# Scores of batches 1 to 3 in quarters of 32 queries over 136 keys, in 64x32 tiles of the array, with the global keys laid between the local ones

## Chip, cores and metric

The kernel runs on one core of one Trainium2 chip. The metric is device time in microseconds for one execution, the median over runs. Lower is better.

## What is computed

Local attention with a few global keys, and behind it a gated two-layer network that also mixes positions:

```python
batch, n_heads, seq, head_dim = (4, 8, 768, 64)
n_global, n_local = (8, 96)
scores = scale * np.matmul(q, k.transpose(0, 1, 3, 2))
rel = pos[:, None] - pos[None, :]
is_global = pos[None, :] < int(n_global)
is_local = (rel >= 0) & (rel < int(n_local))
dist = np.where(is_global & ~is_local, float(n_local), np.abs(rel).astype(np.float32))
scores = np.where(is_global | is_local, scores - slopes * dist, -1000000000.0)
a = np.exp(scores - np.max(scores, axis=-1, keepdims=True))
x = np.matmul(a / (np.sum(a, axis=-1, keepdims=True) + 1e-09), v)
h = np.maximum(x @ w_in, 0.0)
u, v = (h[..., :d_ff // 2], h[..., d_ff // 2:])
v_n = (v - mu) / np.sqrt(var + 1e-06)
v_s = np.einsum('ts,bsd->btd', w_spatial, v_n) + b_spatial[None, :, None]
return (u * v_s) @ w_out
```

A query sees the 8 global keys and the 96 keys up to itself.

## The kernel before

The work is cut into 24 blocks n of 128 queries: 4 batches b of 6 blocks i. Everything is resident in on-chip memory apart from the block's q, k and v, which SP's queue loads (`prep`, L767, and `prep_v`, L785).

For each block, `scores` (L799) multiplies q by k in fp32. A head has 64 channels, and two heads lie on the upper and the lower 64 partitions, so the array is used as four 64x64 tiles: 64 channels by 64 queries (`halves`). A half of 64 queries sees 168 columns of k (`KW`): 64 + 96 local keys and 8 global ones, which stand first for the upper half and last for the lower. The first block of a batch (i = 0) has 128 columns. One block is 16 calls: 4 pairs of heads, 2 halves of queries, 2 heads. They fill four PSUM banks `s`. Then `tensor_tensor_reduce` on DVE adds the bias (`bias`, made in `setup_bias` and its inner function `more`, L674, with huge negative entries for keys that a query must not see) and takes the minimum, and ACT does the exponential.

In batches 1 to 3 the probabilities of the next block are transposed (`turns_of`, in 64-partition tiles of 104 or 128 columns, into `s` banks), copied to `pth`, and multiplied with v (`values`, `p<-pth,vring`, four 64x64 tiles). Scores of the block after that mostly stand right behind the values. In batch 0 the transposes are full 128-wide ones. The network's matmuls (`mlp_v`, `mlp_u`, `mlp_s`, `mlp_o`, all written to PSUM tiles `m`) use the whole 128x128 array. They fill the time in which DVE and ACT work on a block's probabilities.

The order of all of it is made at build time: a recorder (`Recorder`, `Engine.keep`, whose line L45 every recorded instruction carries) collects the operations, and `plan` orders them per engine by a table of ranks (`KEYS`) and by costs per operation (`cost`, `shape_of`, `lengths`). `shape_of` (L283) gives PE's tile shape a number and a cost for entering it. `keep_warm` puts dummy transposes (`m<-ident` and the like) into PE's early gaps.

Of the kernel before, what the change touches and what calls it, by code (L numbers as in the profile page):

```python
# [282 lines left out]
def shape_of(op):  # L283

    if op.eng != "tensor":
        return 0, 0
    if op.call != "together":
        return 0, 149 if op.call == "transpose" else 190
    if op.args[-1][0] == "transpose":
        return 3, 145  # L290
    return (1, 135) if list(op.args[-1][2]["lhsT"].ap)[0][1] <= HALF else (2, 150)


def lengths(op):
# [225 lines left out]
def attn_then_spatial_gating_kernel(  # L520
# [47 lines left out]
    k_own = k[:, :, :, :, KP:KP + P]  # L568
# [76 lines left out]

    def setup_bias():
# [610 lines left out]
```

## Time and profile before

| what | us |
|---|---|
| median of 3 runs (lowest, highest) | 427.72 (427.56, 427.98) |
| the profiled execution's own time | 426.2 |
| its span, first to last instruction | 424.4 |
| PE busy (share of the span) | 411.9 (97%) |
| DVE busy | 284.9 (67%) |
| ACT busy | 196.7 (46%) |
| POOL busy | 91.1 (21%) |

The profiled execution is 1.5 us shorter than the median of the runs, and 1.8 us of its time lie outside the span. PE's records of matmuls overlap, since they are pipelined, so its busy share says that it seldom stood empty and not that it ran at its peak. An fp32 matmul call leaves two records on PE, each with a weight load on PEld: a block's 16 score calls are 32 records. The network's matmuls leave one record each.

### The profile page before, as it was taken

To read this page: it belongs to the slowest core of one execution; us is meant where nothing else is said; L and a number is where in the kernel's file an instruction comes from. 1 tells how busy PE (TensorE), PEld (TensorE's weight loads), DVE (VectorE), ACT (ScalarE), POOL (GpSimd) and SP (SyncE) were. 2 spreads that over 40 slices of the span, in tenths; PEclk is the share of its full clock that TensorE was granted. 3 is DMA by queue.
4 is the path that set the end of the run, shared out by engine and by line. 5 is a ranking of instruction groups with operands and counts; after the bars stand their busy time and mean duration, and the time that the engine had idled before them with its cause. 6 is when DMAs were issued, how large, how long until landed. Compare 5 with 4: busy or idle time off the path is not lost.

```text
span 424.4 us, 11946 instructions
## 1 busy us (share of the span) xinstructions
PE 411.9 (97%) x4845; PEld 365.9 (86%) x4845; DVE 284.9 (67%) x1010; ACT 196.7 (46%) x606; POOL 91.1 (21%) x123
## 2 busy tenths in 40 slices
PE   7899899999999999999999999999999999999994
PEld 6667798998898889899889888899989889899993
DVE  7999998679777776748877727658578423524240
ACT  5689675555636552556553525633353222311111
POOL 2355244731000052320010012241010023410000
PEclk9999999999999999999999999999999999999999
DMA  7998555233434530434462314404041010000102
GB/s 236 404 388 300 209 194 178 98 124 102 169 123 146 178 103 21 148 88 144 134 200 78 136 37 148 148 3 145 14 155 61 26 49 2 2 2 2 74 2 82
DMA packets 18885, 51.46 MB, mean 121 GB/s; under 512 B 1924, under 2 KB 4228, under 8 KB 18180
## 3 DMA queue, kind: packets, MB, share of 16 engines
q1 hardware_dynamic: 18820, 50.60, 34.7%
q8 instruction: 40, 0.66, 0.6%
q14 instruction: 25, 0.20, 0.2%
HBM read 44.30 MB, written 6.29 MB: 119 GB/s over the span
## 4 chain that ended last, share of the span: by engine, by line
PE 86%; DVE 10%; ACT 2%; issue 1%; DMA 0%; SPq 0%; DVEq 0%; ACTq 0%
PE m L45 70%; PE s L45 9%; PE p L45 8%; DVE pth L45 4%; DVE pr L45 2%; DVE w_in_l L45 1%; ACT pr L45 1%; DVE w_in_h L45 1%; DVE ev L45 1%; DVE c L45 0%; DMA nraw<-in_n_local_dram 0%; DVE bias L45 0%; DVE xtl L45 0%; DVE rc L45 0%; ACT w_t_h L45 0%
## 5 line engine op out<-in xcount | busy, mean ns | idle before, releaser
L45 ACT ACTIVATE pr<-pr,mn 128x168 f32<-128x168 f32 (+1 forms) x192 | 80.0, 418 | 10.5 <-DVE mn L45 10.3
L45 DVE CUSTOM_DVE_ANT_0 pr<-s,bias 128x168 f32<-128x168 f32 (+1 forms) x192 | 51.3, 319 | 13.3 <-ACT c L45 7.2
L45 ACT ACTIVATE ev<-m 128x512 f32<-128x512 f32 (+1 forms) x40 | 23.5, 589 | 59.2 <-PE m L45 50.5
L45 ACT ACTIVATE gh<-ev 128x384 fp32r<-128x384 f32 x32 | 16.8, 525 | 54.6 <-DVE ev L45 54.5
L45 DVE TENSOR_TENSOR ev<-m,b_bc 128x384 f32<-128x384 f32 x32 | 17.8, 556 | 35.1 <-PE m L45 35.1
L45 PE MATMUL m<-w_t_h,vnh 128*128 128x384 f32 x192 | 40.0, 340 | 0.0
L45 PE MATMUL m<-w_t_l,vnh 128*128 128x384 f32 x192 | 39.8, 337 | 0.0
L45 PE MATMUL p<-pth,vring 64*64 64x64 f32 (+4 forms) x1968 | 39.4, 221 | 0.0
L45 DVE TENSOR_SCALAR pr<-pr,rc 128x168 f32<-128x168 f32 (+1 forms) x134 | 38.7, 345 | 0.6
L45 PE MATMUL m<-w_t_h,vnl 128*128 128x384 f32 x192 | 39.0, 336 | 0.0
L45 PEld LDWEIGHTS p<-pth,vring 64*64 64x64 f32 (+3 forms) x1968 | 36.0, 135 | 2.8 <-issue 0.7
L45 POOL TENSOR_TENSOR vnl<-ev,vnh 128x512 fp32r<-128x512 f32 x24 | 31.2, 1301 | 29.0 <-ACT vnh L45 13.6
L45 DVE BATCH_NORM_STATS2 st<-ev 128x6 f32<-128x512 f32 x24 | 16.5, 690 | 29.7 <-ACT ev L45 29.5
L45 ACT ACTIVATION_READ_ACCUMULATOR pr<-pr,mn 128x1 f32 x192 | 36.0, 188 | 0.0
L45 PEld LDWEIGHTS m<-w_t_h,vnh 128*128 128x128 f32 x192 | 33.7, 188 | 1.5 <-issue 1.2
L45 PEld LDWEIGHTS m<-w_t_l,vnh 128*128 128x128 f32 x192 | 34.1, 188 | 0.3
L45 PEld LDWEIGHTS m<-w_t_h,vnl 128*128 128x128 f32 x192 | 34.0, 188 | 0.2
L45 PE MATMUL s<-k,q 64*64 64x168 f32 (+1 forms) x768 | 32.5, 306 | 0.6 <-DMA k<-in_k_dram 0.5
L45 ACT ACTIVATE u<-m 128x384 f32<-128x384 f32 x28 | 13.7, 491 | 37.3 <-PE m L45 37.2
L45 PE MATMUL m<-w_out_h,gh 128*128 128x512 f32 (+1 forms) x96 | 31.0, 397 | 0.0
L45 ACT ACTIVATE pth<-s 104x512 f32<-104x512 f32 (+2 forms) x37 | 17.6, 531 | 28.5 <-PE s L45 28.0
L45 PE MATMUL m<-w_out_l,gh 128*128 128x512 f32 (+1 forms) x96 | 29.8, 390 | 0.0
(117 smaller groups left out, 788.4 us busy)
## 6 DMA issues: line engine op xcount, KB each, us to landing
vring<-in_v_dram SPq DMA_DIRECT2D x15, 768.0 KB, 4.4
k<-in_k_dram SPq DMA_DIRECT2D x20, 480.0 KB, 5.7
q<-in_q_dram SPq DMA_DIRECT2D x24, 256.0 KB, 4.0
out_dram<-ev SPq DMA_DIRECT2D x23, 256.0 KB, 2.0
vring<-in_v_dram SPq DMA_DIRECT2D x5, 1024.0 KB, 5.1
u<-in_moe_w_in_dram SPq DMA_DIRECT2D x6, 512.0 KB, 6.7
gh<-in_moe_w_spatial_dram SPq DMA_DIRECT2D x6, 384.0 KB, 7.5
k<-in_k_dram SPq DMA_DIRECT2D x4, 256.0 KB, 4.4
```

The costliest lines, as they stand in the source:

```text
L45: getattr(self.real, call)(*args, **kw)
```

## The change

Past the first batch (b > 0) and past the first block of a batch (i > 0), which makes 15 of the 24 blocks, the scores are taken in quarters of 32 queries (`fours`), each with 136 columns (`QW`), in eight 64x32 tiles. A block has 32 calls in place of 16. For that the host lays the 8 global keys between the local ones (`GAT` says where), so that a quarter's keys are one run of columns: the first or the last 136 of its half's 168. The bias and the rows of v are laid in the same way. The 32 columns that a quarter leaves out hold what was there before, and the bias masks them. DVE and ACT still read 168 columns. k gets a second copy of a block's own keys in memory, so that the load for a batch's first block is one contiguous run per partition. `shape_of` knows a fifth tile shape, and the table of ranks is new.

```diff
+KALL = KW + HALF + NGMAX
+GAT = (HALF, KP - NGMAX)
+QW = KW - 32
...
-    return (1, 135) if list(op.args[-1][2]["lhsT"].ap)[0][1] <= HALF else (2, 150)
+    w = op.args[-1][2]["lhsT"]
+    if elements(w) < HALF:
+        return 4, 135
+    return (1, 135) if list(w.ap)[0][1] <= HALF else (2, 150)
...
-    tiles = 4 if shape_of(op)[0] == 1 else 2
+    tiles = {1: 4, 2: 2, 4: 8}[shape_of(op)[0]]
+    if tiles == 8:
+        return [4 * elements(kw["rhs"]) * .417 / tiles + 1 for _, _, kw in op.args]
...
-KEYS = {'start': -756.31, ('P', 0): -243.7, ('bias', 0): -495.76, ...
+KEYS = {'start': -867.27, ('P', 0): -293.52, ('bias', 0): -457.54, ...
...
-    k_own = k[:, :, :, :, KP:KP + P]
+    k_own = k[:, :, :, NP * KALL:].rearrange("n t p (g c) -> n t p g c", c=P)
...
+    halves = [slice(64 * j, 64 * j + 64) for j in range(2)]
+    fours = [slice(32 * j, 32 * j + 32) for j in range(4)]
...
-            ts(out=rel[HALF:P], in0=rel[HALF:P], scalar1=-float(HALF + NGMAX), scalar2=None, op0=ALU.add)
+            for ps, cs, by in ((halves[0], slice(0, GAT[0]), NGMAX), (halves[1], slice(0, GAT[1]), HALF + NGMAX), (halves[1], slice(GAT[1], KW), HALF)):
+                ts(out=rel[ps, cs], in0=rel[ps, cs], scalar1=-float(by), scalar2=None, op0=ALU.add)
             kept(far, rel)
-            nc.vector.tensor_copy(out=far[0:HALF, 0:NGMAX], in_=glob[0:HALF, 0:NGMAX])
-            nc.vector.tensor_copy(out=far[HALF:P, KW - NGMAX:KW], in_=glob[HALF:P, 0:NGMAX])
+            for ps, at in zip(halves, GAT):
+                nc.vector.tensor_copy(out=far[ps, at:at + NGMAX], in_=glob[ps, 0:NGMAX])
...
-        nc.load(out=kt[:, :, cs], in_=k[b, i, :, :, cs])
+        if i:
+            nc.load(out=kt, in_=k[b, i, :, 0:NP * KALL].rearrange("p (g c) -> p g c", c=KALL))
+        else:
+            nc.load(out=kt[:, :, KP:KP + P], in_=k_own[b, i])
...
+        if b and i:
+            where = [(zs, los[y // 2], (KW - QW) * (y % 2), QW) for y, zs in enumerate(fours)]
+        else:
+            where = [(zs, lo, 0, W) for zs, lo in zip(halves, los)]
...
-                    ("matmul", (sp[x // 2 * 2 + j][zs, x % 2],), dict(
-                        lhsT=qt[s_, g + x, zs], rhs=kt[s_, g + x, lo:lo + W], start=True, stop=True,
+                    ("matmul", (sp[x // 2 * 2 + j][zs, x % 2, at:at + w],), dict(
+                        lhsT=qt[s_, g + x, zs], rhs=kt[s_, g + x, lo + at:lo + at + w], start=True, stop=True,
                     ))
-                    for x in range(PAIRS) for zs, lo in zip(halves, los) for j, s_ in enumerate(halves)
+                    for x in range(PAIRS) for zs, lo, at, w in where for j, s_ in enumerate(halves)
```

The first place is PE at one of the 15 blocks (n = 17): the last values (`p<-pth,vring`, out of `values`), the first scores (`s<-k,q`), the last scores and the first matmul of the network (`m<-`). Before, in calls:

```order
L45 MATMUL p_1_118<-pth_3_128,vring_0_92 64x64
L45 MATMUL p_1_118<-pth_2_127,vring_0_92 64x64
L45 MATMUL s_0_100<-k_1_115,q_1_114 64x168
L45 MATMUL s_1_101<-k_1_115,q_1_114 64x168
...
L45 MATMUL s_2_104<-k_1_115,q_1_114 64x168
L45 MATMUL s_3_105<-k_1_115,q_1_114 64x168
...
L45 MATMUL m_1_135<-w_t_h_72,vnh_0_133 128x384
```

With the change:

```order
L49 MATMUL p_1_118<-pth_3_128,vring_0_92 64x64
L49 MATMUL p_1_118<-pth_2_127,vring_0_92 64x64
L49 MATMUL s_0_100<-k_1_115,q_1_114 32x136
L49 MATMUL s_1_101<-k_1_115,q_1_114 32x136
...
L49 MATMUL s_2_104<-k_1_115,q_1_114 32x136
L49 MATMUL s_3_105<-k_1_115,q_1_114 32x136
...
L49 MATMUL m_1_135<-w_t_h_72,vnh_0_133 128x384
```

The two rows of a pair of banks alternate: 8 calls into `s_0` and `s_1` and 8 into `s_2` and `s_3` before, 16 and 16 now. What stands ahead of and behind them is the same. In 11 of the 15 blocks the scores follow values directly, as here, and in 4 a matmul of the network; it is 11 and 4 in both kernels.

The second place is PE at the end of batch 0: the last scores of the first block of batch 1 (n = 6, `s<-k,q`, 128 columns) and the values of block 4 before, of block 5 now. Before:

```order
L45 MATMUL s_2_104<-k_0_94,q_0_93 64x128
L45 MATMUL s_3_105<-k_0_94,q_0_93 64x128
L45 MATMUL m_0_129<-xth_0_116,w_in_h_68 128x384 x4
L45 MATMUL m_0_129<-xtl_0_117,w_in_h_68 128x384 x4
...
L45 MATMUL m_1_135<-xth_0_116,w_in_l_69 128x384 x4
L45 MATMUL p_0_87<-pth_3_128,vring_0_92 64x64 x2
```

With the change:

```order
L49 MATMUL s_2_104<-k_0_94,q_0_93 64x128
L49 MATMUL s_3_105<-k_0_94,q_0_93 64x128
L49 MATMUL p_1_118<-pth_2_127,vring_0_92 64x64 x2
L49 MATMUL p_1_118<-pth_0_119,vring_0_92 64x64 x2
L49 MATMUL p_1_118<-pth_2_127,vring_0_92 64x64 x2
```

Before, 24 matmuls of the network stood between these scores and the next values; now the values follow at once, in the same 64x64 tiles. Elsewhere in batch 0 as many stretches of scores or values stand between matmuls of the network as before.

The third place is DVE at the start, in `setup_bias` (`ev` holds distances, `nf` and `nwide` the two sizes that are loaded). Before:

```order
L45 TENSOR_SCALAR ev_2_97<-ev_0_95 128x128
L45 TENSOR_SCALAR ev_0_95<-ev_0_95 64x168
L45 TENSOR_SCALAR ev_1_96<-ev_2_97 128x128
L45 TENSOR_TENSOR ev_2_97<-ev_2_97,ev_1_96 128x128
L45 CAST nf_64<-nraw_63 128x4
```

With the change:

```order
L49 TENSOR_SCALAR ev_2_97<-ev_0_95 128x128
L49 TENSOR_SCALAR ev_0_95<-ev_0_95 64x64
L49 TENSOR_SCALAR ev_1_96<-ev_2_97 128x128
L49 TENSOR_SCALAR ev_0_95<-ev_0_95 64x96
L49 TENSOR_TENSOR ev_2_97<-ev_2_97,ev_1_96 128x128
L49 TENSOR_SCALAR ev_0_95<-ev_0_95 64x72
L49 CAST nf_64<-nraw_63 128x4
```

One operation on 64x168 has become three, all ahead of the cast that waits for the loaded sizes. From there DVE's rows are the same up to its 108th operation without the readings of minima (33 us in the trace before), and up to the 145th but for one copy that stands later (52 us). Behind that, operations of batch 0 change places.

## Rows read from the trace of the kernel before

**Rows 1.** Page, parts 1 and 2: PE's busy time, and the granted clock by slices.

```profile
PE 411.9 (97%) x4845; PEld 365.9 (86%) x4845; DVE 284.9 (67%) x1010; ACT 196.7 (46%) x606; POOL 91.1 (21%) x123
...
PEclk9999999999999999999999999999999999999999
```

**Rows 2.** Page, part 4: the chain that ended last, by engine.

```profile
PE 86%; DVE 10%; ACT 2%; issue 1%; DMA 0%; SPq 0%; DVEq 0%; ACTq 0%
```

**Rows 3.** The chain in order of time, 50 to 66 us: start, length, what.

```profile
51.44 0.61 DVE pth L45
...
52.08 0.64 ACT w_in_h L45
...
52.76 1.67 PE m L45 x8
```

**Rows 4.** Busy time of each engine in stretches: length, then busy time and count.

```profile
50.00:60.00 10.00, 9.63 (x135) 8.79 (x135) 9.97 (x38) 7.50 (x28) 3.50 (x5) 1.00 0.57 197
60.00:80.00 20.00, 20.00 (x214) 17.75 (x213) 16.53 (x49) 9.53 (x25) 11.80 (x19) 1.00 0.52 173
...
55.00:418.00 363.00, 363.00 (x4261) 327.10 (x4260) 232.63 (x808) 156.34 (x477) 68.76 (x97) 1.00 0.28 94
```

**Rows 5.** Timeline of PE, 215 to 245 us: start, length, operation, count.

```profile
217.48 1.63 PE L45 MATMUL p<-pth,vring 64*64 64x64 f32 x96
218.93 1.32 PE L45 MATMUL s<-k,q 64*64 64x168 f32 x32
220.18 1.33 PE L45 MATMUL m<-w_t_h,vnh 128*128 128x384 f32 x6
...
236.89 1.06 PE L45 MATMUL s<-k,q 64*64 64x128 f32 x32
237.88 0.50 PE L45 MATMUL m<-w_out_h,gh 128*128 128x512 f32 x1
```

**Rows 6.** Timeline of PE at 218.9 us; the form's row of the groups by shape.

```profile
218.93 0.33 PE L45 MATMUL s<-k,q 64*64 64x168 f32 x4
...
L45 PE MATMUL s<-k,q 64*64 64x168 f32 x640 | 27.4, 306 | 0.1
```

**Rows 7.** Timeline of PE at 332 us: values followed by the network's matmuls.

```profile
332.64 1.63 PE L45 MATMUL p<-pth,vring 64*64 64x64 f32 x96
334.20 0.73 PE L45 MATMUL m<-w_out_h,gh 128*128 128x512 f32 x2
```

**Rows 8.** Timeline of PE at 270 us: scores that follow the network's matmuls.

```profile
270.05 1.37 PE L45 MATMUL s<-k,q 64*64 64x168 f32 x32
271.36 1.21 PE L45 MATMUL m<-w_in_h,xth 128*128 128x512 f32 x4
```

**Rows 9.** Timeline of PE, 57 to 62.5 us: scores of block 6, the network, values.

```profile
57.00 1.10 PE L45 MATMUL s<-k,q 64*64 64x128 f32 x32
58.03 0.97 PE L45 MATMUL m<-xth,w_in_h 128*128 128x384 f32 x4
58.84 0.87 PE L45 MATMUL m<-xtl,w_in_h 128*128 128x384 f32 x4
59.55 0.86 PE L45 MATMUL m<-xth,w_in_l 128*128 128x384 f32 x4
...
61.66 0.87 PE L45 MATMUL m<-xth,w_in_l 128*128 128x384 f32 x4
62.46 0.74 PE L45 MATMUL p<-pth,vring 104*64 104x64 f32 x18
```

**Rows 10.** Timeline of DVE, 1.2 to 2.7 us; the form that is split.

```profile
2.06 0.29 DVE L45 TENSOR_TENSOR ev<-ev,ev 128x128 f32<-128x128 f32 x1
2.53 0.17 DVE L45 CAST nf<-nraw 128x4 f32<-128x4 int32 x1 [0.17 <-DMA nraw<-in_n_local_dram]
...
L45 DVE TENSOR_SCALAR ev<-ev 64x168 f32<-64x168 f32 x1 | 0.2, 245 | 0.0
```

**Rows 11.** Waits of PE in the whole span: us in total, times, longest.

```profile
PE m L45 <- DVE w_in_h L45: 0.8, 1, 0.8
...
PE s L45 <- DMA k<-in_k_dram: 0.5, 1, 0.5
```

More of the change, by code (lines that the diff above doesn't have):

```diff
@@ new lines @@
+KEYS = {'start': -867.27, ('P', 0): -293.52, ('bias', 0): -457.54, ('S', 0, 0): 117.44, ('S', 0, 1): 32.55, ('bias', 1): -353.15, ('W', 0): 163.14, (0, 'I', 1, 0, 'D'): -101.27, (0, 'I', 1, 0): 175.43, (0, 'I', 1, 1, 'D'): -118.74, (0, 'I', 1, 1): -496.55, (0, 'I', 1, 2, 'D'): 426.95, (0, 'I', 1, 2): -929.4, (0, 'I', 1, 3, 'D'): -56.42, (0, 'I', 1, 3): -729.56, ('P', 1): 44.92, ('A', 0, 0): 31.01, ('S', 1, 0): 292.15, ('A', 0, 1): 32.37, ('S', 1, 1): 191.12, ('W', 1): -52.65, (0, 'I', 0, 0, 'D'): 519.03, (0, 'I', 0, 0): -397.11, (0, 'I', 0, 1, 'D'): 34.05, (0, 'I', 0, 1): -426.25, (0, 'I', 0, 2, 'D'): -652.05, (0, 'I', 0, 2): 40.21, (0, 'I', 0, 3, 'D'): 678.29, (0, 'I', 0, 3): -488.02, (0, 'T', 0, 'D'): 239.05, (0, 'T', 0): 434.77, (0, 'T', 1, 'D'): 164.33, (0, 'T', 1): -378.84, ('P', 2): 237.52, ('A', 1, 0): 542.25, ('S', 2, 0): -315.72, ('A', 1, 1): -16.74, ('S', 2, 1): -678.53, ('W', 2): 472.46, (0, 'V', 0): 243.31, (0, 'V', 0, 1): 514.52, (0, 'B', 0, 'D'): 348.43, (0, 'T', 2, 'D'): -477.37, (0, 'T', 2): 8, (0, 'T', 3, 'D'): -514.78, (0, 'T', 3): 367.32, ('P', 3): 70.86, ('A', 2, 0): 76.9, ('S', 3, 0): -48.54, ('A', 2, 1): 176.59, ('S', 3, 1): -234.65, ('W', 3): 321.59, (0, 'V', 1): -541.83, (0, 'V', 1, 1): 769.32, (0, 'T', 4, 'D'): 777.5, (0, 'T', 4): 161.97, (0, 'T', 5, 'D'): 283.23, (0, 'T', 5): 582.81, ('P', 4): 478.34, ('A', 3, 0): -55.87, ('S', 4, 0): -185.32, ('A', 3, 1): -312.44, ('S', 4, 1): 174.03, ('W', 4): 725.46, (0, 'V', 2): -324.52, (0, 'V', 2, 1): 524.45, (0, 'U', 0, 0): 279.73, (0, 'U', 0, 1): -14.95, (0, 'U', 0, 2): -523.11, (0, 'U', 0, 3): 150.89, ('P', 5): 271.55, ('A', 4, 0): 102.65, ('S', 5, 0): 340.48, ('A', 4, 1): -77.76, ('S', 5, 1): 422.81, ('W', 5): -295.83, (0, 'V', 3): 39.87, (0, 'V', 3, 1): 160.15, ('P', 6): 810.12, ('A', 5, 0): -70.54, ('S', 6, 0): 300.42, ('A', 5, 1): -303.35, ('S', 6, 1): -312.38, ('X', 6): 619.54, ('W', 6): 568.19, (0, 'V', 4): 106.52, (0, 'V', 4, 1): -53.55, (0, 'Q', 0, 0, 'D'): 803.09, (0, 'Q', 0, 0): 282.92, (0, 'Q', 0, 1, 'D'): 644.81, (0, 'Q', 0, 1): -37.9, (0, 'Q', 1, 0, 'D'): 515.9, (0, 'Q', 1, 0): -729.12, (0, 'Q', 1, 1, 'D'): 744.84, (0, 'Q', 1, 1): 524.95, (0, 'Q', 2, 0, 'D'): -3.18, (0, 'Q', 2, 0): 347.89, (0, 'Q', 2, 1, 'D'): 334.39, (0, 'Q', 2, 1): 529.1, (0, 'Q', 3, 0, 'D'): 312.17, (0, 'Q', 3, 0): 669.31, (0, 'Q', 3, 1, 'D'): 476.77, (0, 'Q', 3, 1): 215.52, (0, 'V', 5): 326.36, (0, 'V', 5, 1): 878.07, (0, 'U', 1, 0): 446.52, (0, 'U', 1, 1): -401.8, (0, 'U', 1, 2): -240.88, (0, 'U', 1, 3): -361.67, ('P', 7): -133.62, ('S', 7): -124.2, ('A', 6): 458.46, ('W', 7): 425.24, (0, 'G', 0, 0): 111.28, (0, 'G', 0, 1): -106.55, (0, 'G', 0, 2): -62.13, (0, 'G', 0, 3): -681.6, (0, 'O', 0, 0): -171.12, (0, 'O', 0, 1): -54.57, (0, 'O', 0, 2): -241.65, ('P', 8): 589.81, ('S', 8): 329.27, ('A', 7): -494.02, ('W', 8): 462.82, (0, 'G', 1, 0): -102.75, (0, 'G', 1, 1): -241.66, (0, 'G', 1, 2): 348.43, (0, 'G', 1, 3): 25.58, (0, 'O', 1, 0): 102.38, (0, 'O', 1, 1): -651.72, (0, 'O', 1, 2): 392.92, (1, 'V', 0): 750.75, ('P', 9): 735.69, ('S', 9): -386.14, ('A', 8): 18.34, ('W', 9): 768.94, (1, 'V', 1): 408.63, (1, 'V', 2): 330.48, ('P', 10): 429.18, ('S', 10): -65.32, ('A', 9): 753.35, ('W', 10): -60.75, (1, 'U', 0): -379.94, ('P', 11): 462.75, ('S', 11): -224.69, ('A', 10): -108.93, ('W', 11): 482.78, (1, 'V', 3): -477.25, ('P', 12): 523.29, ('S', 12): 242.7, ('A', 11): 421.4, ('W', 12): -130.09, (1, 'V', 4): -202.46, (1, 'V', 5): -412.22, (1, 'U', 1): -88.69, ('P', 13): -482.55, ('S', 13): -486.17, ('A', 12): 286.33, ('W', 13): 197.83, (1, 'G', 0): 739.78, (1, 'O', 0): -297.25, ('P', 14): 506.53, ('S', 14): -469.6, ('A', 13): 8.27, ('W', 14): 584.7, (1, 'G', 1): 135.14, (1, 'O', 1): -163.98, (2, 'V', 0): -0.65, ('P', 15): 389.52, ('S', 15): -543.74, ('A', 14): 770.18, ('W', 15): 777.83, (2, 'V', 1): -30.52, (2, 'V', 2): 91.61, ('P', 16): 571.3, ('S', 16): -602.74, ('A', 15): -207.48, ('W', 16): 580.51, (2, 'U', 0): -339.38, ('P', 17): -639.75, ('S', 17): -153.37, ('A', 16): 432.54, ('W', 17): 779.98, (2, 'V', 3): 303.69, ('P', 18): 391.67, ('S', 18): -166.23, ('A', 17): 523.15, ('W', 18): 529.44, (2, 'V', 4): -315.29, (2, 'V', 5): -471.31, (2, 'U', 1): -158.36, ('P', 19): -496.26, ('S', 19): -541.13, ('A', 18): 220.71, ('W', 19): 386.25, (2, 'G', 0): 208.28, (2, 'O', 0): -431.85, ('P', 20): 524.77, ('S', 20): 534.76, ('A', 19): -670.06, ('W', 20): 729.2, (2, 'G', 1): 28.74, (2, 'O', 1): -227.44, (3, 'V', 0): -165.26, ('P', 21): 384.99, ('S', 21): -670.42, ('A', 20): 321.07, ('W', 21): -99.33, (3, 'V', 1): -440.92, (3, 'V', 2): 58.61, ('P', 22): -104.27, ('S', 22): -511.8, ('A', 21): 47.5, ('W', 22): -545.09, (3, 'U', 0): 134.85, ('P', 23): 217.95, ('S', 23): -475.79, ('A', 22): 365.67, ('W', 23): 514.52, (3, 'V', 3): -149.15, ('A', 23): 253.37, (3, 'V', 4): -621.86, (3, 'V', 5): -547.27, (3, 'U', 1): -463.38, (3, 'G', 0): -430.69, (3, 'O', 0): -66.07, (3, 'G', 1): 90.63, (3, 'O', 1): 326.58}
@@ L764, in attn_then_spatial_gating_kernel @@
     ring = {}
-    halves = [slice(64 * j, 64 * j + 64) for j in range(2)]
     def prep(n):
         b, i = divmod(n, NB)
-        cs = slice(0, None) if i else slice(KP, KP + P)
         qt = work.tile([P, NP, P], F32, name="qt", tag="q", bufs=2)
@@ L1218 @@
                 first = _np.broadcast_to(a[:, :1, :, :, :NGMAX], a.shape[:4] + (NGMAX,))
-                before = _np.concatenate([a[:, :1], a[:, :-1]], axis=1)[:, :, :, :, P - KP + NGMAX:]
-                a = _np.concatenate([first, before, a, first], axis=4)
+                local = _np.concatenate([_np.concatenate([a[:, :1], a[:, :-1]], axis=1)[:, :, :, :, P - KP + NGMAX:], a], axis=4)
+                near, mid, far = local[..., :HALF], local[..., HALF:HALF + KP - NGMAX], local[..., HALF + KP - NGMAX:]
+                a = _np.concatenate([x.reshape(x.shape[:3] + (-1,)) for x in (_np.concatenate([near, first, mid, first, far], axis=4), a)], axis=3)
         elif name == "v":
@@ L1225 @@
             lower, upper = (at + _np.arange(x - KW + NGMAX, x) for x in (HALF, P))
-            keys = [_np.maximum(_np.concatenate(x, axis=1), 0) for x in ((shared, lower), (upper, shared))]
+            keys = [_np.maximum(_np.concatenate([x[:, :n], shared, x[:, n:]], axis=1), 0) for x, n in ((lower, HALF), (upper, KP - NGMAX))]
             def rows(x, h, n):
```

1 line of the change is left out of this document (removed).

## The prediction

> **What bounds the kernel now.** I read the page first: PE is busy for 411.9 of 424.4 us, at a granted clock of 9 tenths or more (2.4 GHz) in every slice [rows 1], and the chain that ended last runs 86% over PE [rows 2]. Then the chain in order of time: DVE and ACT set the pace up to 52.8 us, where PE takes over [rows 3]. The stretches say the same: from 55 to 418 us PE has something in flight all the time [rows 4]. So a microsecond that PE saves past 55 us comes off the end; one that it saves earlier is lost in waits for DVE. All 15 changed blocks lie past 80 us. What PE pays for a block must be read from the distance between starts on its timeline, since records overlap.
>
> **Scores, by rounds.** A block's 32 records of 168 columns take from 218.93 to 220.18, 1.25 us; those of a 128-column block from 236.89 to 237.88, 0.99 us [rows 5]. Both run on four tiles, so in 8 rounds of four, and the 0.26 us between them are 40 columns: 6.5 ns a column over 8 rounds. With 136 columns the same 8 rounds would take 0.99 + 8 x 0.0065 = 1.04 us up to the next matmul; one round is 136 x 6.5 / 8 = 111 ns and a few more between rounds, some 115 ns. The change has 64 records on eight tiles, which is again 8 rounds. So a block gains 1.25 - 1.04 = 0.21 us, if eight tiles run together as four do.
>
> **The spread of a round.** The four records of the first round span 0.33 us where one lasts 0.306 [rows 6]: the starts lie about 0.02 us apart over three steps, some 7 ns a step. Eight tiles have four steps more, 0.03 us, paid once at a block's end. That leaves 0.18 us, and 15 x 0.18 = 2.7 us.
>
> **The new change of tile shape.** Before, values and scores share 64x64 tiles, and the scores start 1.45 us behind the first values (217.48 to 218.93) [rows 5]. Where the network's 128x128 matmuls follow the same 96 values, it is 1.56 us [rows 7]: leaving the shape costs 0.11. Scores that come from another shape take 1.31 us (270.05 to 271.36) [rows 8] and not 1.25: the first weight load is exposed, 0.05. In 11 of the 15 blocks the scores follow values directly, and now they have another shape: 11 x 0.16 = 1.8 us lost. The other 4 come from the network's matmuls, as before, and pay nothing new. Going from scores to the network was a change of shape already. I take 0.16 for a change that no row shows (64 to 32 columns, with the row halves kept). The bounds are 0 below (no drain between these two shapes) and, above, 0.30: the 0.16 with a second first load and a second spread for four more tiles.
>
> **The stretch saved in batch 0.** Scores of block 6 now run straight into values. Before, PE went from scores to 24 matmuls of the network and back [rows 9]. Coming in, the first four take 0.81 us (58.03 to 58.84) against 0.71 for the next; going out, the last four take 0.80 (61.66 to 62.46): 0.10 and 0.10 (rounded up from 0.09). Leaving the scores, 0.11, and the first load of the values, 0.05, go too. In sum 0.36 us, past 55 us and thus on the path. The bounds are 0 (values of block 5 wait for their copies of the probabilities, the cover being 16 score calls) and 0.4.
>
> **The start.** One DVE operation of 0.245 us becomes three, smaller ones, ahead of the cast that waits 0.17 us for a load [rows 10]. Two more operations lie between 0 (hidden behind that wait and between dependent operations) and 2 x 0.245 = 0.5 us. I take 0.05, since the idle 0.17 and the gaps hold most of it; DVE sets the pace here, so what isn't hidden counts.
>
> **The rest.** DVE and ACT read 168 columns as before. The contiguous k load for a batch's first block is one load of each batch; PE waited for k once, 0.5 us [rows 11], at the start, where DVE's bias is later than the scores: 0, at most 0.3 gained. In batch 0 the new ranks move operations of DVE, ACT and POOL. PE has work ready from 55 us, and DVE has 3.5 of 20 us free in 60 to 80 [rows 4], so I take 0, with 0.8 as the upper bound, the longest wait of PE for a result of DVE there is [rows 11], and as much below, where the handover at 52.8 comes earlier.
>
> **The sum.** -2.7 + 1.8 - 0.36 + 0.05 = -1.2 us. On the profiled execution that is 426.2 - 1.2 = 425.0. The median of the runs shown stands 1.5 above it, so 427.72 - 1.2 = 426.5.
>
> **A rule against it.** The 96 records of the values start within 1.45 us, 15 ns apart, each with its own weight load [rows 5]; the new scores want 115 / 8 = 14.4 ns. The Trainium skill, in TensorE: Matmul & The Clock Gate (Wait — 56ns, not 53.3ns?), says that starts of matmuls never come closer than about 25 ns, however small they are. By that a block would need 64 x 25 = 1.6 us in place of 0.92 in rounds, 15 x 0.68 = 10 us more, some 436.7 us. The trace disagrees: 15 ns is measured, for matmuls in four separate tiles.
>
> **The rivals.**
>
> *Eight tiles don't run together.* No row shows more than four. If they have to take turns by fours, a block needs 16 rounds of 115 ns in place of 8: 15 x 0.92 = 13.8 us more, 440.3 us. Between the two it is a matter of the round: each 10 ns cost 15 x 8 x 0.010 = 1.2 us. From 125 ns there is no gain, from about 132 ns it is slower by over 0.2%. Against it speaks that twice as many columns of the array are not asked for, only split in narrower tiles, and that loads carry 32 columns in place of 64. For it, that four column groups must be fed from the same 64 partitions where there were two. 0.13 for all of it past 132 ns, the skill's 25 ns included.
>
> *Issue at the pace of the values.* If 15 ns is as fast as pairs of load and matmul can start, a round takes 121 ns and 0.7 us go: 427.2, within the bound. Against it: the four starts of a round lie only 7 ns apart. 0.15.
>
> *No drain between the two tile widths.* Both have the same row halves. If loads of the next shape go ahead as they do between values and scores now, the 1.8 us stay: 424.7. 0.12. The Trainium skill, in TensorEngine Tiling (Array Packing) (Key Properties), says that changing the tiling mode, not just the tile, drains the engine; by it this rival falls, but no row here has that pair of shapes.
>
> *A new wait in batch 0.* Less of the network's work stands between scores, transposes and values there, and DVE is full up to 60 us [rows 4]. One wait of the 0.8 seen gives 427.3. 0.12.
>
> That the change doesn't do what it says I leave out: the order of calls shows the 32 calls, and the same neighbours.
>
> **How the numbers follow.** The forecast has 0.48, and 426.5 is its time. A measurement of this kernel can tell some 0.2%, 0.86 us, from no change: 426.86 and 428.58 are the borders. The forecast's own spread (0 to 0.5 at the start, 0.8 in batch 0) leaves 0.44 below the first border and 0.04 above. Faster: 0.44 + 0.12 (no drain) + 0.02 (a small wait) = 0.58. Same: 0.04 + 0.15 (issue) + 0.09 (wait) = 0.28. Slower: 0.13 and 0.01 of the waits. The range reaches down to the rival without a drain with a little of the bounds below, 424.5, and up to the same-sided cases, 428.0; outside it are the slow eight tiles and little else.
>
> **What would show it.** On the timeline, 64 records of scores and the next matmul 1.04 + 0.03 + 0.05 = 1.12 us behind the first one, and values to scores 1.56 in place of 1.45 in 11 blocks. PE should stay full from 55 us on, and the handover should come near 52.8. The forecast is wrong if scores stand 1.3 us or more apart (tiles in turns), if values to scores stays at 1.45 (no drain), or if a wait of PE past 55 us appears.

## The result and the profile after

The change makes the kernel slower: the median of 5 runs is 430.46 us (430.12 to 431.3), and 427.72 for the kernel before in the same session. The ratio is 1.0071, 95% interval 1.0051 to 1.0092, so about 3.0 us. The forecast was 426.5 within 424.5 to 428.0. The profiled execution took 431.04 us with a span of 429.0, against 426.2 and 424.4.

PE has 480 more matmuls, 32 for each of 15 blocks, and as many more weight loads [rows 1]. The DMA queue q8 carries instructions, in packets of about 16 kB: 44 of them, where the page of the kernel before has `q8 instruction: 40, 0.66, 0.6%`. From the page of the changed kernel:

```profile
PE 411.2 (96%) x5325; PEld 364.7 (85%) x5325; DVE 287.9 (67%) x1017; ACT 199.7 (47%) x609; POOL 85.5 (20%) x115
...
q8 instruction: 44, 0.72, 0.7%
```

An ordinary changed block, on the timeline of PE (start, length, operation, count):

```profile
188.26 1.63 PE L49 MATMUL p<-pth,vring 64*64 64x64 f32 x96
189.82 1.22 PE L49 MATMUL s<-k,q 64*32 64x136 f32 x64
190.97 0.45 PE L49 MATMUL m<-xth,w_in_h 128*128 128x384 f32 x1
```

Values to scores takes 1.56 us (1.45 before [rows 5]) and scores to the next matmul 1.15 (1.25 before [rows 5], 1.31 behind the network [rows 8]). At three of the 15 blocks, in the scores or right behind them, PE stops with work in hand, which no stretch of the kernel before shows past 55 us [rows 4]. Timeline of all engines, rows of PE and PEld:

```profile
127.40 1.13 PE L49 MATMUL s<-k,q 64*32 64x136 f32 x56
...
129.51 0.44 PE L49 MATMUL s<-k,q 64*32 64x136 f32 x8 [0.98 <-issue]
129.52 0.15 PEld L49 LDWEIGHTS s<-k,q 64*32 64x32 f32 x7 [1.27 <-issue]
129.88 0.30 PEld L49 LDWEIGHTS m<-w_t_h,vnh 128*128 128x128 f32 x2 [0.21 <-issue]
```

and timeline of PE at the other two:

```profile
257.99 1.22 PE L49 MATMUL s<-k,q 64*32 64x136 f32 x64
259.14 0.62 PE L49 MATMUL m<-xth,w_in_h 128*128 128x384 f32 x2
260.36 0.51 PE L49 MATMUL m<-xth,w_in_h 128*128 128x384 f32 x2 [0.60 <-issue]
...
334.26 1.22 PE L49 MATMUL s<-k,q 64*32 64x136 f32 x64
336.20 0.50 PE L49 MATMUL m<-w_out_h,gh 128*128 128x512 f32 x1 [0.72 <-ACT pr L49]
```

In the first, 56 score matmuls start, then nothing for over a microsecond, then the last 8, which use the same q, k and banks as those before them. "issue" is time in which the engine waited for nothing that the profile shows. The block takes 129.88 - 127.40 = 2.48 us in place of 1.15. The next matmul of the last one stands 1.94 us behind the scores and not 1.15. The profile puts it down to a result of ACT, but it lies at the same place in PE's stream as the other two (below). In the middle one two starts lie 0.94 us apart where 0.18 is usual. That is 1.3 + 0.8 + 0.8 = 2.9 us, nearly the whole loss.

The waits of PE (engine, releaser: us in total, times, longest) hold the three stops and two more things that rows 11 did not have, a longer wait for k and one of 1.6 us for `w_in_h`, both ahead of 55 us:

```profile
PE s L49 <- DMA k<-in_k_dram: 1.9, 2, 1.4
...
PE m L49 <- ACT w_in_h L49: 1.6, 1, 1.6
...
PE s L49 <- issue: 1.0, 1, 1.0
...
PE m L49 <- ACT pr L49: 0.7, 1, 0.7
...
PE m L49 <- issue: 0.6, 1, 0.6
```

**Where PE's records stand when it stops.** Counts of PE's records (matmuls, weight loads and its sequencer's few) up to each stop past 57 us:

```
changed kernel   128.3 us  3265 = 12 x 256 + 193
                 259.4 us  7361 = 28 x 256 + 193
                 335.2 us  9409 = 36 x 256 + 193
```

A packet of q8 has 16384 bytes. With 256 instructions to a packet an instruction has 64, and the 960 records that PE has more would fill 3.75 packets; there are 4 more. In a window around the first stop the DMA view shows one packet and nothing else (queue: packets, MB, share):

```profile
q8 instruction: 1, 0.02, 5.2%
```

It starts at 126.97 us and takes 1.08 us; PE goes on at 129.51. At the other two stops a packet starts at 257.54 and 333.92. So a first theory, **C**: the instructions come in pieces of 256, and PE stops where it has used up a piece before the next is there. A dense stretch now has 48 records of transposes, 192 of values and 128 of scores, 368 in some 3.5 us; before it was 304.

**Start and batch 0.** A good mark is the first 16 transposes of batch 1: the work of PE ahead of them is the same in both kernels. Timeline of PE, before and after:

```profile
81.03 0.71 PE L45 MATMUL s<-ident,pr 64*128 64x64 f32 x16
```

```profile
83.53 0.72 PE L49 MATMUL s<-ident,pr 64*128 64x64 f32 x16
```

They come 2.5 us later; from them to the end of the span it is 343.4 us before and 345.5 after. So the two profiled executions lie 4.6 us apart, where the medians lie about 3 apart. Two theories for the first part: **A**, the new order of the work; **B**, the new layout of the keys, behind whose first load the others land later (the first v load took 10.7 us and not 8.9 in the lists of DMA issues).

### The profile page after: what moved, and what is told of

It reads as the page before. It is cut to its first block, busy times and chain, and to the rows that moved or that the text cites. A ratio compares the mean times of both kernels' runs of the same rounds, so it can differ in the third digit from the quotient of the medians.

```text
span 429.0 us, 12893 instructions
## 1 busy us (share of the span) xinstructions
PE 411.2 (96%) x5325; PEld 364.7 (85%) x5325; DVE 287.9 (67%) x1017; ACT 199.7 (47%) x609; POOL 85.5 (20%) x115
## 4 chain that ended last, share of the span: by engine, by line
PE 86%; DMA 6%; DVE 4%; ACT 1%; issue 1%; SPq 1%; ACTq 0%
PE m L49 69%; PE s L49 9%; PE p L49 8%; DMA vring<-in_v_dram 3%; DVE pth L49 2%; DMA k<-in_k_dram 2%; DMA gh<-in_moe_w_spatial_dram 1%; DVE pr L49 1%; ACT pr L49 1%; SPq L49 1%; DVE w_in_h L49 0%; DVE w_in_l L49 0%; DVE c L49 0%; ACT w_in_h L49 0%; ACT pth L49 0%
## 5 line engine op out<-in xcount | busy, mean ns | idle before, releaser
L49 PE MATMUL s<-k,q 64*32 64x136 f32 (+2 forms) x1248 | 31.2, 287 | 2.9 <-DMA k<-in_k_dram 1.9
L49 PE MATMUL m<-xth,w_in_h 128*128 128x384 f32 x128 | 29.7, 347 | 2.2 <-ACT w_in_h L49 1.6
L49 PEld LDWEIGHTS s<-k,q 64*32 64x32 f32 (+1 forms) x1248 | 23.8, 114 | 7.1 <-issue 3.7
```

The costliest lines, as they stand in the source:

```text
L49: getattr(self.real, call)(*args, **kw)
```

## The experiments

Times are medians. Behind them stands the ratio to the kernel before on the same chip with its 95% interval; it comes from all runs and can differ from the ratio of two medians by 0.1%. Three dots mark lines of an edit that are left out (the planner's costs, mostly).

**1. The kernel before again.** No edit.

> The kernel before, unchanged, for a second profile of it. Three theories on the 2.7 us: A, the new order of work costs time in batch 0; B, the new layout of k makes the first loads land later (w_in's first piece 1.1 us, v's first load 1.5 us later than in the trace before); C, the 64 extra records of a block's scores outrun PE's supply of instructions (two stops of about 1 us). A and C: the first v load lands near 12.7 us again, since nothing differs. B: the same here, 12.7. If instead it lands anywhere between 12.5 and 14.2, the lateness of the loads in the changed kernel's one profile is scatter from execution to execution. Time 427.7.

426.8 us, 0.9998 (0.9983 to 1.0012); no stop of this kind, but a wait of 1.1 us for a load of v at 69.8 us; first transposes at 81.88 us, so this mark scatters by about 1 us. The first piece of `w_in` landed at 7.36 us and v's first load at 12.12, as in the first trace (7.53 and 12.68); in the changed kernel it was 8.59 and 14.19. So the late loads are no scatter: in the kernels with the new layout `w_in` landed at 8.3 to 9.3 us.

**2. The layout alone**, with the old scores and the old order:

```
-        if b and i:
+        if False:
             where = [(zs, los[y // 2], (KW - QW) * (y % 2), QW) for y, zs in enumerate(fours)]
...
-KEYS = the new ranks
+KEYS = the old ranks
```

> The kernel before with the new layout of keys, values and bias alone (own keys contiguous, two more DVE operations at the start); scores in 64x64 halves, order as before. B: v's first load lands near 14.2 us, and the time is 1 to 2 us above before, 429. A and C: within 0.3 us of before, 427.7.

427.46 us, 1.0017 (0.9995 to 1.0038). First transposes at 81.44. The loads do land later, and the time hardly shows it.

**3. The new scores with the old ranks and old costs.**

```
-    if elements(w) < HALF:
-        return 4, 135
+    if elements(w) < HALF:
+        return 1, 135
...
-KEYS = the new ranks
+KEYS = the old ranks
```

> The changed kernel with the table of ranks and the planner's costs of before, so the order of work is the old one (the load queue's exactly, PE's through batch 0), and scores in quarters. C: the steady gain of 0.9 us, less one stop of about 1 us for each place where PE runs out of instructions: 427 to 429, and the trace shows PE idle inside or just behind a block's scores with nothing awaited. A: 426.8, since the old order is back. B: 0.9 less and 1.5 more, 428.3.

440.83 us, 1.0327 (1.0302 to 1.0351): a miss. The ranks gave another order in batch 1, where PE was left with 12 matmuls of the network between two blocks. Its waits:

```profile
PE m L49 <- ACT xth L49: 4.2, 2, 4.0
PE m L49 <- DVE xth L49: 2.6, 1, 2.6
```

Behind them the granted clock fell (0.72 in the stretch from 180 to 192 us, matmuls of the network 0.43 us apart and not 0.23). It tells nothing of A, but it has a stop inside scores at 144.9 us, at record 3777 = 14 x 256 + 193, and one of 0.3 us at 270 us, at record 7361 = 28 x 256 + 193.

**4. The new order and layout, with the old halves.**

```
-        if b and i:
+        if False:
...
-        return [4 * elements(kw["rhs"]) * .417 / tiles + 1 for _, _, kw in op.args]
+        return [8 * QW * .417 / tiles + 2 for _ in op.args]
```

> The changed kernel with scores in 64x64 halves again, everything else and the order of all engines as in the changed kernel (three rows differ). A: all of the loss is in the order, so 430 to 431. C: no stop past 55 us, 427.7 to 428.7. B: 429.

427.76 us, 1.0029 (1.0007 to 1.0051). No stop past 55 us; first transposes at 83.66. Between this and the change lie 0.0042 of 427.7 us, 1.8 us: some 0.7 gained by the scores and 2.9 lost in stops would make 2.2, and the difference lies within the intervals. Against number 2, the same halves in the old order, it is 0.3 us, less than the intervals can tell.

**5. The stream shifted by 118 records.** In the changed kernel the 59 dummy transposes of `keep_warm` become matmuls of 32 columns, two records longer each:

```
-        op.ways = ((nc.tensor, "transpose", (ps_p.have[place, False][:, 0:P], ident, ident), {}),)
+        op.ways = ((nc.tensor, "matmul", (ps_p.have[place, False][:, 0:32],), dict(lhsT=ident, rhs=ident[:, 0:32], start=True, stop=True)),)
```

> The changed kernel, nothing left out; only the 59 filler instructions that keep TensorE warm early in the program are now matmuls of 32 columns in place of transposes of the same length, which puts 2 more records each into PE's instruction stream: everything past them stands 118 records later in the stream, at the same place in time. Theory C (PE's instructions arrive in pieces of 256 records, and a stretch of transposes, values and scores uses one up faster than the next one arrives): the stops at 128, 259 and 335 us vanish, and others of about 1 us appear where a border of 256 records now falls behind a dense stretch: by the records of the changed kernel's trace near 210, 289 and 306 us, perhaps near 137. Each still lies at the same place of a piece of 256 (record 193 of it). Time within 1.5 us of the changed kernel's 430.5. Rival D (these three blocks wait for something of their own, a buffer or a result of ACT): the stops stay at 128, 259 and 335 us, and the time stays at 430.5.

444.77 us, 1.0395 (1.0377 to 1.0413). The time was a miss: the dummies are not of the same length. Such a matmul leaves two records on PE, and on the timeline 17 records take 12.23 - 8.60 = 3.63 us, 0.21 us each; a transpose leaves one. They filled PE at the start, and the first transposes of batch 1 came at 95.62 us:

```profile
8.60 3.81 PE L49 MATMUL p<-ident 128*128 128x32 f32 x17
12.23 0.67 PE L49 MATMUL p<-ident,pr 128*128 128x128 f32 x2
```

In the changed kernel 12 transposes take 1.47 us, 0.12 each:

```profile
12.19 1.47 PE L49 MATMUL m<-ident 128*128 128x128 f32 x12
```

But the stops moved as C says. Less the 12.1 us of the start, those past 100 us are at 138.5, 177, 213, 293 and 312 us, none at 128, 259 or 335; C had named the neighbourhood of 137, 210, 289 and 306, and had not named the one at 177, of 0.3 us. They sum to 4.3 us; from the first transposes to the end it is 347.3 us. All five are at record 193 of a piece. D falls.

**6. Shifted by 150**, with one more dummy in 8 gaps:

```
-                    out.extend(make(best[1]) for _ in range(int((gap - 300) // (112 if last > WARM_COLD else 216))))
+                    out.extend(make(best[1]) for _ in range(1 + int((gap - 300) // (112 if last > WARM_COLD else 216))))
```

> As the run with a shift of 118 records, with one filler more in each of 8 gaps: the stream past them stands 150 records later. Nothing left out. Theory C: by the records of the changed kernel's trace this is a place where no piece of 256 records is used up in under 2.6 us (the pieces that led to stops took 2.0 to 2.5), so no stop of PE past 55 us or one short one near 209 us; the 2.8 us of the three stops come back, less what the 8 fillers may cost at the start: 427.5 to 428.3. Rival D (the three blocks wait for something of their own): stops at 128, 259 and 335 us again, 430.5.

443.87 us, 1.0381 (1.0358 to 1.0403), from the same start. Two stops, 0.4 and 0.9 us, the first near the 209 us named (225.5 less 14.3 us of a later start), the second, at 305.0, not named; none at the old places. From the first transposes to the end it is 344.0 us, 3.3 less than with 118, and the stops differ by 2.9. The time was a miss again, by the dummies at the start.

**7. The new scores in the old order, call for call.** As number 3, with costs that leave PE's order as it was:

```
+    if elements(op.args[-1][2]["lhsT"]) < HALF:
+        return [(y % 2) * (4 * KW * .417 / 4 + 2) for y, _ in enumerate(op.args)]
```

> The changed scores (64 records in 64x32 tiles) and the new layout of the keys, with the order of the work of the kernel before on PE call for call. Nothing left out. Theory A (the new order costs 1.7 to 2 us in batch 0): the first 16 transposes of batch 1 start at 81.0 to 82.2 us as in the kernel before, in place of 83.5, and from there to the end it takes 342.5 us (343.4 less the 0.9 that the scores give) and about 1 us for each stop of PE's instruction supply: 426.5 with no stop, 427.5 with one, 429.5 with three. Theory B (the layout's later loads cost it): the first transposes stay near 83.5 us, the time at 428 to 430.5.

429.42 us, 1.0045 (1.0029 to 1.0061); first transposes at 82.70; stops of 0.5, 1.2 and 0.7 us at 115.5, 145.2 and 259.3. The first transposes come later than theory A had it; in this execution DVE and ACT handed over to PE at 54.34 us. So the old order takes off about 1.1 us of the 3.0, of which 0.5 are shorter stops, and most of the rest is stops: -0.7 + 2.4 = 1.7 of the 1.9 us.

**8. The layout with the first k load in pieces.** As number 2, a batch's own keys stored with gaps, which the host fills up:

```
-    k_own = k[:, :, :, NP * KALL:].rearrange("n t p (g c) -> n t p g c", c=P)
+    k_own = k[:, :, :, NP * KALL:].rearrange("n t p (g c) -> n t p g c", c=KALL)[:, :, :, :, 0:P]
```

> The kernel before with the new layout of the keys alone, but with a batch's own keys stored with gaps, so that the first block's load of k again fetches four pieces of 512 bytes for each partition in place of one of 2048. Nothing left out. Theory B (the contiguous first load of k is what makes the loads behind it land later): the first piece of w_in lands at 7.4 to 7.6 us as in the kernel before, not at 8.6 to 9.3 as with the layout, and the first v load at 12.1 to 12.7 and not at 13.1 to 14.2; time 427.1. Rival (the loads land later for another reason, the shared tables or the larger array of keys): 8.6 us or later again, and 427.5.

427.52 us, 0.9986 (0.9969 to 1.0003). The first piece of `w_in` still landed at 8.51 us and v at 13.52: contiguity is not what delays them. And with the same late loads the kernel is no slower than before. B falls as a cost that can be measured; why the loads land later stays open.

**9. Halves in 4 of 15 blocks, so that no piece is used up fast**, in the old order of number 7:

```
-        if b and i:
+        if b and i and n not in (10, 13, 15, 19):
```

> The changed scores with the old order of the work call for call, but in 4 of the 15 blocks (10, 13, 15, 19) the scores go back to halves of 64 queries and 168 columns: 64 records there in place of 128. Nothing left out. The four blocks are picked from the trace of the run in the old order, so that every piece of 256 PE records that ends past 57 us is used up slowly: counted from 48 records ahead of its start, the fastest takes 4.0 us, where all pieces that led to a stop but one took under 3.6. Theory C (instruction supply): no stop of PE past 55 us; the 2.5 us of stops come back, some 0.2 us go into the four wider blocks: 427.0, about 0.999 of the kernel before. Rival D (a stop belongs to a block with 64 records and comes with some of them at random): 11 of 15 blocks are left, so about 1.8 us of stops, 428.7.

426.56 us, 0.9989 (0.9968 to 1.001). Among PE's waits there is no "issue" any more; the block in which number 7 stopped runs through, and a pause of 0.2 us in one block (at 114.2 us, at record 193 of a piece as well) is all that is left of the stops. Timeline of PE in number 7:

```profile
144.31 1.16 PE L49 MATMUL s<-k,q 64*32 64x136 f32 x61
146.37 0.42 PE L49 MATMUL s<-k,q 64*32 64x136 f32 x3 [0.90 <-issue]
146.72 0.73 PE L49 MATMUL m<-w_in_h,xtl 128*128 128x512 f32 x2
```

and here, the same block with the same 64 records:

```profile
142.52 1.22 PE L49 MATMUL s<-k,q 64*32 64x136 f32 x64
143.67 0.73 PE L49 MATMUL m<-w_in_h,xtl 128*128 128x512 f32 x2
```

**10. The counterpart: halves in four other blocks.**

```
-        if b and i and n not in (10, 13, 15, 19):
+        if b and i and n not in (7, 19, 22, 23):
```

> The counterpart: as the run with blocks 10, 13, 15 and 19 in halves, the same number of halves and of records, but in blocks 7, 19, 22 and 23. Nothing left out. By the same count five pieces of 256 records are used up in 2.3 to 2.6 us. Theory C: stops of 0.4 to 1.4 us each at about 116, 134, 172, 221 and 288 us (plus the length of the stops before), 4 to 5 us in sum: 431 to 432. Rival D: as many stops as in the run with the other four, the same time within 0.5 us.

432.9 us, 1.0119 (1.0091 to 1.0148), against 426.56 for the same work. Five stops, as many as named. The first, and PE's waits:

```profile
117.52 1.15 PE L49 MATMUL s<-k,q 64*32 64x136 f32 x59
119.91 0.43 PE L49 MATMUL s<-k,q 64*32 64x136 f32 x5 [1.24 <-issue]
120.27 0.50 PE L49 MATMUL m<-w_out_l,gh 128*128 128x512 f32 x1
```

```profile
PE s L49 <- issue: 3.7, 5, 1.3
```

They stand at 118.4, 138.2, 176.2, 226.3 and 293.7 us. Named were 116, 134, 172, 221 and 288; this execution's first transposes came 2.3 us later than in number 7, and each stop adds its length to the next: the first three alone make 116 + 2.3 = 118.3, 134 + 2.3 + 1.5 = 137.8 and 172 + 2.3 + 2.1 = 176.4. The sum is 5.0 us, in a profiled execution of 435.66 us whose granted clock was 0.66 from 20 to 30 us; the median is lower. In the ratios the two kernels lie 1.3% or 5.6 us apart, so the stops are most of it. This run, against number 9, settles C.

**11. Number 9 with the keys in pieces of number 8.**

> As the run with blocks 10, 13, 15 and 19 in halves, and a batch's own keys stored with gaps, so that the first k load of a batch is again four pieces of 512 bytes for each partition. Nothing left out. If the stored gaps are what made the layout's run with pieces 0.3% faster than the layout's run without, this is 0.3% below the run without gaps, 425.7, and the first version below the kernel before by more than the bound. If those two differ by scatter (the loads of w_in and v landed equally late in both), it is the same as the run without gaps, 427.0.

427.2 us, 1.0004 (0.9979 to 1.0029): the same as number 9 within the intervals, so nothing shows a gain by the gaps. With the records of number 9 it has a stop of 0.3 us where that one pauses, at 114.6 us.

No version is below the kernel before by more than can be measured. Number 9, the nearest, keeps 11 of the 15 blocks in quarters.

## Why the prediction was wrong

**The rounds: right but for 0.03 us.** Predicted was 1.12 us from scores to the next matmul, 1.15 is measured. Eight tiles run together, so the rival that had them take turns falls. The 64 records start within 0.95 us, 15 ns apart on average, but not evenly. In the trace of the block at 189.82 us eight start 6 to 7 ns apart, and the next eight follow 115 to 116 ns behind them; only in the last rounds the starts lie further apart. So a round takes the 115 ns worked out, and the rival with issue at the pace of the values falls too. What is longer is the first round, 140 ns, and the spread of the last, 0.11 us where 0.05 was taken. Over 15 blocks the 0.03 us takes 0.5 us off the gain. The Trainium skill's 25 ns between starts (TensorE: Matmul & The Clock Gate, Wait — 56ns, not 53.3ns?) doesn't hold for matmuls in separate tiles here.

**The change of tile shape: right.** Values to scores takes 1.56 us, as worked out. The rival without a drain falls. The Trainium skill says in TensorEngine Tiling (Array Packing), Key Properties, that a new tiling mode drains the engine; the trace agrees, with 0.11 us more than between two 64x64 shapes [rows 5].

**The sum of both.** -2.7 + 1.8 = -0.9 was predicted, and with the 0.5 it is -0.4. Straight from the rows it is -0.5: 11 blocks behind values gain 0.10 and lose 0.11, and 4 behind the network gain 1.31 - 1.15 each. From the first transposes to the end it was 343.4 us before; it is 345.5 - 2.9 = 342.6 in the changed kernel without its stops, and 344.0 - 1.4 = 342.6 in number 6: about -0.7, in the direction and nearly the size of the sum.

**"PE has work ready from 55 us": the step that failed.** The sum asked of each step what data it waits for, and how long it runs, and took for granted that a PE with operands at hand runs. The sign that the prediction had named, a wait of PE past 55 us, is what appeared. The added records of a block (64 of matmuls and weight loads) were costed as array time alone. They are also instructions that must be fetched, and in a stretch of transposes, values and scores they come at 100 records in a microsecond. At the three stops a packet took 0.9 to 1.4 us to move, and PE went on only 2.3 to 2.8 us after it had started; over all 21 stops it is 2.2 to 2.9. And past 57 us no packet of any trace starts more than 297 records ahead of the record at which PE can stop for it. To see what decides, I counted the time that PE takes for a piece and the 48 records ahead of it, 304 in all, stops taken out. All 18 pieces of the traces for which it was under 3.4 us led to a stop, of 0.3 to 1.5 us; of 11 between 3.4 and 4.1 us three did, of 0.3 to 0.5 us, and of the slower ones none. The kernel before has none under 6.1, the change three, at 2.4, 2.4 and 2.8. That it has none is in part luck of where its pieces end: its dense stretches have 304 records, and one from the first transposes at 216.65 to the network's matmuls at 220.18 takes 3.5 us. What sets the moment at which a packet starts stays open. The term was +2.9, and the prediction had 0. The q8 row stood on the page before; with the 15 ns of the values beside it the term could have been named, but no row priced it.

**Batch 0: taken as 0, its size is open.** Taken was 0, with 0.8 above. The handover that should come near 52.8 us does, at 52.90 (the chain in order of time):

```profile
52.22 0.64 ACT w_in_h L49
52.85 0.04 issue
52.90 0.44 PE m L49
...
65.87 1.03 PE s L49 x32
66.90 2.02 PE p L49 x64
```

But PE has more of its work still before it. From there to the first transposes it is 83.53 - 52.90 = 30.6 us; before it was 81.03 - 52.76 = 28.3 [rows 3]. Number 4, with the same order, has 30.6 too, and numbers 2, 7 and 9, with the old one, 28.3 to 28.5. So DVE's chain hands over at the same time, but what PE could do meanwhile was left for later: 2.3 us in the trace. The medians show less: number 7 against the change is 1.0045 to 1.0071, 1.1 us, of which 0.5 are stops, and number 4 against number 2 is 0.3. The intervals overlap in both, so some 0.3 to 0.6 us is likely, none is possible, and that the 0.8 was too low isn't shown. The stretch of batch 0 that was saved is there (scores at 65.87, values right behind them), but its 0.36 can't be told apart from this.

**The start and the layout: small, as said.** The loads land later by a microsecond or more, which wasn't foreseen, but numbers 8 and 11 show no cost of it beyond the scatter.

So -0.7 + 2.9 and 0.3 to 0.6 make 2.5 to 2.8 us, where 3.0 is measured (2.2 to 3.9 by the interval). Of the rivals, the one on the other side of zero asked for slow tiles; the loss came from elsewhere.

## What to carry to other kernels

Count instructions as well as array time: where tiling splits work into many short matmuls, look how long an engine takes for one packet of its instruction queue, and compare that with the time from a packet's start to the moment at which the engine can go on (2.2 to 2.9 us here). A stop with "issue" as its cause inside a run of like matmuls, whose place moves when instructions are added far ahead, is this one. And when an order is replanned, ask of the moment at which the bound passes from one engine to another not only when it comes, but how much work is left behind it.

## What the runs showed of the hardware

PE's stops of this kind all lie at one place of a piece: 21 of them in seven kernels (3 in the change; 2, 5, 2, 3, 5 and 1 in numbers 3, 5, 6, 7, 10 and 11), each at record 193 of 256. Two kernels with the same work, numbers 9 and 10, differ by 6.3 us in their medians; 5.0 us of it are stops, set by where the piece borders fall. Matmuls in eight 64x32 tiles start 6 to 7 ns apart within a round, and a round of 136 fp32 columns takes 115 to 116 ns, as was estimated from the rows of four 64x64 tiles. An fp32 matmul of 32 columns on the whole array left two records of 0.21 us each on PE, where a transpose of 128 columns left one of 0.12.
